# Linear attention and an MLP in one kernel: decay row through TensorE, matmuls of the identity in the opening, group 0 in smaller pieces, other load gates and order keys

## The chip, the cores and the metric

One core of a Trainium2 chip. The metric is the device time in microseconds (us) of one execution; the median of some runs stands for a kernel.

## What is computed

Inputs r, k, v of shape (4, 8, 768, 48), f32, and w, u of shape (8, 48). For each of 4 batches and 8 heads, over 768 steps:

```python
cur = outer(u * k_t, v_t)
y_t = r_t @ (state + cur)
state = w[:, None] * state + outer(k_t, v_t)
```

y, seen as 3072 tokens of 384 columns, goes through an MLP: h = x @ w_in (384 x 2048), a gate g (h where h >= 1, 0 where h <= -1, (h + 1)^2 / 4 between), and out = g @ w_out (2048 x 384), f32.

## The kernel before

Time is cut into 6 chunks of 128 steps. A group is one chunk of two batches, so there are 12 groups (g = 0 to 11) of two units each; a unit is 128 tokens. For a group, SP loads R, K and V (L268, L345). Four products follow (L273 to L313): Rs = R * Wup and Ks = K * Wdn, where Wup and Wdn are powers of w by the row's place in the chunk, KU = K * u, RKU = R * KU. `usum` adds RKU up by head (L318), and V2 (L320) is V times that sum. TensorE turns Rs and Ks (T, copied out as TT; from group 5 on by DMA transposes), multiplies them to A, which VectorE masks to AT (L385), and makes Y (from AT, V and the bf16 state) and Sp (the state's update). y = Y + V2 (L412) is turned to xT (TensorE for groups 0 to 2, a DMA transpose from group 3 on).

The MLP takes a group of 256 tokens in four quarters q: `mm1` is 12 matmuls into the PSUM tile hp (L487), ScalarE makes relu (L499) and square (L503), VectorE the gate (L507). Two hp tiles exist, so the third quarter waits for the first one's gate. `mm2` (L521) multiplies the gates by w_out into op, `o` copies op out, `out` stores it. TensorE's other results share four PSUM banks.

All operations are declared with `op` (L156): the engines that may run it with their assumed costs, a key, and what it needs, makes and uses. The loop from L564 on emits them one after the other: of the operations that could start within 0.25 us of the earliest, by assumed times, that with the lowest key on the same engine. Each engine runs its instructions in that emitted order and waits at each for what it really needs. Assumed times and `LOAD_AFTER` (L161) shape the order alone; real waits come from the tiles' buffers.

The opening: `w_row` and `u_row4` are set by memset and then partly loaded (L82 to L86); ScalarE takes the logarithm (L176), VectorE spreads it over the partitions (L179), ScalarE makes Wup and Wdn (L185, L188). w_col is loaded by columns (L92) and squared 7 times on VectorE (L192), for the state's decay wCm. Group 0's products go in halves of 384 columns, one per unit; its Rs and Ks are fixed to VectorE (L312), for groups 1 and 2 the planner chooses between GpSimd and VectorE, later groups use GpSimd.

The weights go in four pieces each through GpSimd's queue, cast to bf16 (L220, L226). `gate_on` (L216) is a 1x1 copy on GpSimd that reads a loaded tile and so holds back the pieces behind it: w_in 0 and 1 behind group 0's second R, w_in 2 and 3 behind group 1's K, w_out 0 and 1 behind group 2's R, w_out 2 and 3 behind group 2's K (L213, L214).

Of the kernel before, what the change touches and what calls it, by code (L numbers as in the profile page):

```python
# [22 lines left out]
def kernel(  # L23
# [53 lines left out]
    w_row = const.tile([P, DM], F32, name="w_row")  # L77
# [12 lines left out]
    for j in range(2):  # L90
        src = bass.AP(tensor=w.tensor, offset=w.offset + j * D, ap=[[1, D], [2 * D, NP]])
        nc.scalar.dma_start(out=w_col[j * HP : j * HP + D, :], in_=src)  # L92
# [28 lines left out]
    lw_row = const.tile([P, DM], F32, name="lw_row")  # L121
    lw = const.tile([P, DM], F32, name="lw")
# [23 lines left out]
    }  # L146
    FLEX, XDMA, TDMA, VCAST = 3, 3, 5, 12
# [30 lines left out]
    def lw_spread(e):  # L178
        nc.vector.stream_shuffle(lw, lw_row, [0] * QUAD)  # L179
# [4 lines left out]
    def wup(e):  # L184
        nc.scalar.activation(Wup.rearrange("p h d -> p (h d)"), lw, AF.Exp, scale=up_col, bias=0.0)  # L185

    def wdn(e):
        nc.scalar.activation(Wdn.rearrange("p h d -> p (h d)"), lw, AF.Exp, scale=dn_col, bias=0.0)  # L188
# [10 lines left out]
    op("w_row", (("NET", 0.0, 3.6),), -99, None)  # L199
    op("u_row4", (("NET", 0.0, 4.0),), -99, None)  # L200
    op("w_col", (("NET", 0.0, 5.0),), -99, None)
    op("lw_row", (("ACT", 0.55),), -98, lw_ln, ["w_row"])
    op("lw", (("DVE", 0.5, 0.08),), -98, lw_spread, ["lw_row"])
    op("u_bc", (("DVE", 0.5, 0.08),), -75, u_spread, ["u_row4"])
    op("exps", (("ACT", 1.28),), -98, lambda e: nc.scalar.preload_act_table_set("exp_and_others"), ["lw_row"])
    op("Wup", (("ACT", 0.53, 0.08),), -97, wup, ["lw", "exps"])
    op("Wdn", (("ACT", 0.53, 0.08),), -96, wdn, ["Wup"])
    op("w_power", (("DVE", 0.6),), -50, w_power, ["w_col"])
    op("wCm", (("ACT", 0.5),), -49, w_spread, ["w_power"])


    NW = 4
    GATE_IN = {0: ("R", 0, 1), 2: ("K", 1, 1)}  # L213
    GATE_OUT = {0: ("R", 2, 1), 2: ("K", 2, 1)}  # L214
    for i in range(NW):
# [10 lines left out]
        def w_out_go(e, i=i):  # L226
            n = slice(i * nF // NW, (i + 1) * nF // NW)
# [24 lines left out]
    for g in range(nG):  # L252
# [4 lines left out]
        for j0, j1 in parts:  # L257
# [5 lines left out]
            for i, (x, what) in enumerate(((r, "R"), (k, "K"))):  # L263

                def load(e, g=g, j0=j0, j1=j1, x=x, what=what):
                    if j0 == 0:
                        tiles[what, g] = loads.tile([P, UNITS * H, D], F32, name=what, tag=what)
                    nc.sync.dma_start(out=tiles[what, g][:, j0 * H : j1 * H, :], in_=source(x, g, j0, j1))  # L268

                op(f"load {what}{tag}", (("DMA", 0.9 * n, 1.35),), tl + i * 0.3, load, LOAD_AFTER.get((what, g), [f"load R{tag}"] if i else []),  # L270
                   [(what, (what, g))] if j0 == 0 else [], [(what, g)])
# [23 lines left out]
            pool_or_dve = (("POOL", 0.89 * n, 0.06, "PORT"), ("DVE", 0.03 + 0.49 * n, 0.05, "PORT")) if early_g else (("POOL", 0.89 * n, 0.06, "PORT"),)  # L295
            pool_only = (("POOL", 0.89 * n, 0.06, "PORT"),)
            first = j0 == 0
            for i, (what, needs) in enumerate(
# [11 lines left out]
                where = pool_or_dve if i < 2 or g in (0, 1, 2) else pool_only  # L310
                if g == 0 and i < 2:
                    where = (("DVE", 0.52, 0.05, "PORT"),)  # L312
# [25 lines left out]
        if g < VCAST:  # L338
# [8 lines left out]
            op(f"loadV{g}", (("DMA", 1.8, 1.35),), (-78 if g == 0 else t0 - 4 + 0.7 + shift("load", g)), load_v32, LOAD_AFTER.get(("V", g), [f"load K{g}.0"] if g else ["load K0.1"]), [("VF", ("VF", g))], [("VF", g)])  # L347
# [9 lines left out]
        for j in range(UNITS):  # L357
# [86 lines left out]
            if g < TDMA:  # L444
                op(f"T{n}", (("PE", 0.45, 0.17),), ka, t_in, [f"Rs{part}", f"Ks{part}"] + ([f"A{n - 1}"] if n > 3 else []), [("bank", ("T", n))], [("T", n), ("Rs", g), ("Ks", g)])
                op(f"TT{n}", (("ACT", 0.92, 0.1), ("DVE", 0.61, 0.08)) if n < 4 else (("DVE", 0.61, 0.08),), ka + 0.3, t_out, [f"T{n}"], [("TT", ("TT", n))], [("T", n), ("TT", n)])
            else:
                tt = f"KT{g}"
                if j == 0:
                    for i in range(2):  # L450
# [5 lines left out]
                        op(f"{'RK'[i]}T{g}", (("DMA", 1.4, 2.6),), ka - 2 + i, t_dma, [f"{w_}{part}"] + ([f"RT{g}"] if i else []),  # L456
# [21 lines left out]
            if g < XDMA:  # L478
                op(f"X{n}", (("PE", 0.17, 0.17),), ka + 3, x_mm, [f"y{n}"], [("bank", ("X", n))], [("X", n), ("y", n)])
                op(f"xT{n}", (("ACT", 0.38, 0.1),), ka + 3.1, x_out, [f"X{n}"], [] if j else [("xT", ("xT", g))], [("X", n), ("xT", g)])  # L480
            else:
                op(f"xT{n}", (("DMA", 0.5, 2.7),), ka + 3, x_dma, [f"y{n}"], [] if j else [("xT", ("xT", g))], [("y", n), ("xT", g)])

        for q in range(nQ):
            k1 = nQ * g + 3 + q + shift("mm1", g)

            def mm1(e, g=g, q=q):  # L487
                hp = tiles["hp", g, q] = psh.tile([P, FG, TOK], F32, name="hp", tag="h")
                for f in range(FG):
# [11 lines left out]
            def square(e, g=g, q=q):
                tiles["sq", g, q] = moe.tile([P, FG, TOK], F32, name="sq", tag="sq", bufs=2)
                nc.scalar.activation(tiles["sq", g, q], tiles.pop(("pt", g, q)), AF.Square, bias=0.0)  # L503

            def gate(e, g=g, q=q):
                gt = tiles["gt", g, q] = gpool.tile([P, FG, TOK], BF16, name="gt", tag="g")
                nc.vector.scalar_tensor_tensor(  # L507
                    out=gt, in0=tiles.pop(("sq", g, q)), scalar=1.0, in1=tiles.pop(("hp", g, q)), op0=ALU.min, op1=ALU.max
                )

            m = (g, q)
            op(f"mm1 {m}", (("PE", 1.31, 0.17),), k1, mm1, [f"xT{g * UNITS}", f"xT{g * UNITS + 1}", f"w_in{q * NW // nQ}"], [("h", ("hp", m))], [("hp", m), ("xT", g)])
            op(f"relu {m}", (("ACT", 0.93, 0.1),), k1 + 0.2, relu, [f"mm1 {m}"], [("pt", ("pt", m))], [("hp", m), ("pt", m)])
            op(f"square {m}", (("ACT", 0.965, 0.1),), k1 + 0.3, square, [f"relu {m}"], [("sq", ("sq", m))], [("pt", m), ("sq", m)])
            op(f"gate {m}", (("DVE", 1.135, 0.09),), k1 + 0.9 + shift("gate", g), gate, [f"square {m}"], [("g", ("gt", m))], [("hp", m), ("sq", m), ("gt", m)])

        for j in range(UNITS):
            for q in range(nQ):
# [13 lines left out]
                op(f"mm2 {o}{q}", (("PE", 0.65, 0.17),), k2, mm2, [f"gate {(g, q)}", f"w_out{q * NW // nQ}"] + ([f"mm2 {o}{q - 1}"] if q else []),  # L532
# [20 lines left out]
    free = {"POOL": 3.9, "DVE": 3.0, "DMA": 2.5}  # L553
# [10 lines left out]
    while waiting:  # L564
        found = []
        for name, (where, key, fn, needs, makes, uses) in waiting.items():
# [15 lines left out]
            for w in where:  # L582
                e = w[0]
                s = max([start, free.get(e, 0.0)] + [free.get(x, 0.0) for x in w[3:]] + [done[x][0] + HOP[e] if done[x][1] != e else done[x][2 if e == "DMA" else 0] for x in needs])
# [7 lines left out]
        cost = w[1] * (2 if e == "PE" and s < 17 else 1)  # L592
# [52 lines left out]
```

## Time and profile before

| | us |
|---|---|
| median of 3 runs | 198.72 |
| lowest, highest | 198.06, 200.79 |
| the profiled execution | 198.8 |
| its span in the trace | 197.0 |

PE is TensorE's matmuls, PEld its weight loads, DVE VectorE, ACT ScalarE, POOL GpSimd, SP the queue that issues loads and stores. The page cuts the span into 40 slices of 4.9 us; a digit is the busy share in tenths. A timeline row gives the start, the length, the engine, the line, the operation with out<-in, shapes, a count where equal ones are merged, and in brackets the idle time before it and what ended it. A row of windows gives the stretch and its length, the busy time of PE, PEld, DVE, ACT and POOL with the count of instructions, the granted clock of TensorE as a share of 2.4 GHz, the share of the DMA engines and GB/s.

### The profile page before, as it was taken

The numbers are of one execution on the slowest core, as the hardware profiler recorded it, in microseconds if no ns is written. First come the engines' busy times: TensorE is split into PE (matmuls) and PEld (weight loads), VectorE is DVE, ScalarE is ACT, GpSimd is POOL, SyncE is SP. The second block draws the span as 40 slices with busy tenths as digits, with TensorE's granted clock in tenths as the row PEclk, the third lists the DMA queues.
The fourth block names the chain that finished last, engine by engine and source line by source line (L and its number), as shares of the span: only waits on it lengthen the run. The fifth ranks groups of instructions, "written<-read, shape, count | busy, mean of one in ns | idle before, by whom it ended". The sixth has DMA issues, their size and how long they took to land.

```text
span 197.0 us, 4036 instructions
## 1 busy us (share of the span) xinstructions
PE 164.2 (83%) x1602; PEld 119.2 (61%) x1602; DVE 141.5 (72%) x205; ACT 134.6 (68%) x167; POOL 101.4 (51%) x82
## 2 busy tenths in 40 slices
PE   0064768299889989999694799999999999999992
PEld 0043656158667676767473477777777777777751
DVE  4699959966997979594780877797787867644540
ACT  2753398235978699775926698777976878878730
POOL 2303303084799888989974579999965000000000
PEclk9999999579999999999999799999999999999998
DMA  6999999999597999979989969744627311121112
GB/s 121 184 191 205 200 194 212 197 195 188 117 186 134 216 168 191 198 148 195 161 156 192 229 122 205 163 113 79 93 60 134 97 39 32 52 63 40 40 40 80
DMA packets 104226, 27.73 MB, mean 141 GB/s; under 512 B 97544, under 2 KB 104208, under 8 KB 104208
## 3 DMA queue, kind: packets, MB, share of 16 engines
q1 hardware_dynamic: 100064, 24.32, 68.8%
q0 software_dynamic: 3712, 3.15, 9.9%
q8 instruction: 12, 0.20, 0.4%
q10 hardware_dynamic: 432, 0.01, 0.2%
q14 instruction: 6, 0.05, 0.1%
HBM read 20.46 MB, written 4.72 MB: 128 GB/s over the span
## 4 chain that ended last, share of the span: by engine, by line
PE 48%; DMA 16%; DVE 13%; ACT 10%; POOL 5%; issue 4%; SPq 2%; POOLq 0%; DVEq 0%; ACTq 0%
PE op L526 21%; PE hp L492 21%; DMA VF<-in_v_dram 14%; ACT sq L503 4%; ACT pt L499 4%; DVE gt L507 3%; DVE AT L385 2%; PE A L380 2%; DMA R<-in_r_dram 2%; DVE Rs L287 1%; PE Y L407 1%; ACT state_bf L169 1%; ACT V L169 1%; POOL state L427 1%; DVE RKU L293 1%
## 5 line engine op out<-in xcount | busy, mean ns | idle before, releaser
L507 DVE SCALAR_TENSOR_TENSOR gt<-sq,hp 128x1024 bf16<-128x1024 f32 x48 | 58.4, 1216 | 33.0 <-ACT sq L503 32.9
L492 PE MATMUL hp<-xT,w_in_sb 128*128 128x256 bf16 x576 | 73.0, 278 | 9.4 <-DVE gt L507 8.7
L526 PE MATMUL op<-w_out_sb,gt 128*128 128x384 bf16 x384 | 75.6, 334 | 4.9 <-DVE TT L169 4.1
L492 PEld LDWEIGHTS <-w_in_sb 128*128 128x128 bf16 x576 | 57.1, 100 | 22.7 <-issue 11.1
L499 ACT ACTIVATE pt<-hp 128x1024 f32<-128x1024 f32 x48 | 48.9, 1018 | 14.8 <-PE hp L492 14.8
L503 ACT ACTIVATE sq<-pt 128x1024 f32<-128x1024 f32 x48 | 50.8, 1058 | 1.3
L526 PEld LDWEIGHTS <-gt 128*128 128x128 bf16 x384 | 35.1, 99 | 25.8 <-issue 6.9
L385 DVE TENSOR_TENSOR AT<-A,umask 128x512 bf16<-128x512 f32 x48 | 31.1, 683 | 8.7 <-PE A L380 8.5
L427 POOL TENSOR_TENSOR state<-Tm,wCm 128x384 f32<-128x384 f32 x16 | 16.0, 1001 | 13.7 <-DVE Tm L422 13.7
L287 POOL TENSOR_TENSOR Rs<-R,Wup 128x768 bf16<-128x768 f32 x9 | 16.4, 1821 | 7.9 <-DMA R<-in_r_dram 7.9
L169 ACT CAST state_bf<-state 128x384 bf16<-128x384 f32 x20 | 10.2, 508 | 15.0 <-DVE state L424 9.0
L169 ACT CAST V<-VF 128x768 bf16<-128x768 f32 x12 | 10.0, 833 | 14.2 <-DMA VF<-in_v_dram 14.2
L289 POOL TENSOR_TENSOR Ks<-K,Wdn 128x768 bf16<-128x768 f32 x9 | 16.4, 1819 | 0.5 <-PE Y L407 0.5
L293 POOL TENSOR_TENSOR RKU<-R,KU 128x768 f32<-128x768 f32 x9 | 16.3, 1816 | 0.4
L291 POOL TENSOR_TENSOR KU<-K,u_bc 128x768 f32<-128x768 f32 x9 | 16.4, 1823 | 0.0
L323 POOL TENSOR_TENSOR V<-V,diag 128x768 f32<-128x768 bf16 x9 | 13.3, 1477 | 4.7 <-DVE y L414 2.7
L414 DVE TENSOR_TENSOR y<-Y,V 128x384 bf16<-128x384 f32 x24 | 13.2, 551 | 0.3
L169 ACT COPY o_sb<-op 128x384 f32<-128x384 f32 x22 | 10.2, 464 | 4.5 <-PE op L526 4.5
L369 PE MATMUL T<-ident,Rs 128*128 128x128 bf16 x40 | 4.6, 246 | 10.3 <-DVE Rs L287 10.2
L318 DVE TENSOR_REDUCE diag<-RKU 128x16 f32<-128x768 f32 (+1 forms) x13 | 11.5, 886 | 1.4 <-POOL RKU L293 1.3
L407 PE MATMUL Y<-V,AT 128*128 128x48 bf16 x192 | 11.9, 188 | 0.2
L407 PEld LDWEIGHTS <-AT 128*128 128x128 bf16 x192 | 10.2, 99 | 1.3 <-issue 0.6
(59 smaller groups left out, 117.0 us busy)
## 6 DMA issues: line engine op xcount, KB each, us to landing
VF<-in_v_dram SPq DMA_DIRECT2D x12, 384.0 KB, 5.9
out_dram<-o_sb SPq DMA_DIRECT2D x24, 192.0 KB, 2.1
R<-in_r_dram SPq DMA_DIRECT2D x11, 384.0 KB, 5.7
K<-in_k_dram SPq DMA_DIRECT2D x11, 384.0 KB, 6.1
w_in_sb<-in_moe_w_in_dram POOLq DMA_DIRECT2D x4, 384.0 KB, 7.3
w_out_sb<-in_moe_w_out_dram POOLq DMA_DIRECT2D x4, 384.0 KB, 8.5
R<-in_r_dram SPq DMA_DIRECT2D x2, 192.0 KB, 3.6
K<-in_k_dram SPq DMA_DIRECT2D x2, 192.0 KB, 4.1
```

The lines of the kernel that those rows point to most:

```text
L169: nc.scalar.copy(out, in_) if e == "ACT" else engines[e].tensor_copy(out, in_)
L287: engines[e].tensor_mul(part(R_s)[:, :, :, :D], part(R), rep(Wup, j1 - j0))
L289: engines[e].tensor_mul(part(K_s)[:, :, :, :D], part(K), rep(Wdn, j1 - j0))
L293: engines[e].tensor_mul(part(tiles["RKU", g]), part(R), part(tiles["KU", g]))
L385: nc.vector.tensor_mul(tiles["AT", n][:, i], tiles["A", n][i], umask.unsqueeze(1).to_broadcast([P, NP, P]))
L407: nc.tensor.matmul(Y[:, 2 * p + i, :], AT[:, i, p, :], V[:, j * H + 2 * p + i, :], start=(c == 0), stop=True, skip_group_check=True,)
L427: nc.gpsimd.tensor_mul(states[b], tiles.pop(("Tm", n)), wCm)
L492: nc.tensor.matmul(hp[:, f, :], w_in_sb[:, i, n0 : n0 + P], tiles["xT", g][:, i, :], start=(i == 0), stop=(i == nK - 1), skip_group_check= ...
L499: nc.scalar.activation(tiles["pt", g, q], tiles["hp", g, q], AF.Relu, bias=0.5, scale=0.5)
L503: nc.scalar.activation(tiles["sq", g, q], tiles.pop(("pt", g, q)), AF.Square, bias=0.0)
L507: nc.vector.scalar_tensor_tensor(out=gt, in0=tiles.pop(("sq", g, q)), scalar=1.0, in1=tiles.pop(("hp", g, q)), op0=ALU.min, op1=ALU.max)
L526: nc.tensor.matmul(tiles["op", g, j], tiles["gt", g, q][:, f, j * P : (j + 1) * P], w_out_sb[:, n, :], start=(n == 0), stop=(n == nF - 1),)
```

## The change

In the opening w_row becomes one partition. TensorE spreads its logarithm with a matmul against a row of ones, and makes w_col with eight small matmuls; the two w_col loads go. `fill` emits 128x128 matmuls of the identity into a spare hp tile wherever the planner sees TensorE free for over 0.5 us before the first `mm1`. Group 0's `mm1` goes in four pieces (half of the rows of hp by unit), its relu, square and gate in two halves. Rs and Ks of group 0 may run on GpSimd too. The gates are fewer: all of w_in behind group 0's second R, all of w_out behind group 1's K. `TUNE` adds an offset to the key of every kind of operation by group (0 to 3, 10, 11, and m for 4 to 9), `ONLY` fixes the engine of some (index into the list of allowed ones). The assumed costs of loads, transposes and products change. TT, xT of groups 0 to 2 and o may run on either of ScalarE and VectorE.

```diff
-    w_row = const.tile([P, DM], F32, name="w_row")
+    w_row = const.tile([1, DM], F32, name="w_row")
-    nc.vector.memset(w_row, 1.0)
+    nc.scalar.dma_start(out=w_row, in_=bcast(w, 1))
+    nc.vector.memset(ones, 1.0)
-    nc.scalar.dma_start(out=w_row[0:P:QUAD, :], in_=bcast(w, P // QUAD))
...
-        nc.scalar.dma_start(out=w_col[j * HP : j * HP + D, :], in_=src)
...
+    TUNE = {
...
+        'KU': {0: 25.13, 1: 33.08, 2: -2.32, 3: 3.63, 11: 0.46, 'm': 13.06},
...
+        'V': {0: 3.19, 2: -4.04, 3: 0.92, 10: 2.53, 11: -0.93, 'm': 12.34},
...
+    ONLY = {
+        'KU': {1: 1, 2: 1},
+        'Ks': {0: 1, 1: 1, 2: 1},
+        'RKU': {0: 0, 2: 1},
+        'Rs': {0: 1},
+        'TT': {1: 0, 2: 0, 'm': 0},
+        'V2': {0: 0, 1: 0, 2: 1},
+        'o': {1: 0, 10: 1, 11: 0, 2: 0, 3: 0},
+        'w_power': {0: 1},
+        'xT': {0: 0, 1: 0, 2: 1},
+    }
...
-    LOAD_AFTER = {("R", 1): ["w_in1"], ("R", 2): ["w_in3"], ("R", 3): ["w_out3"]}
+    LOAD_AFTER = {("R", 1): ["w_in3"], ("R", 2): ["w_out3"]}
...
-        nc.vector.stream_shuffle(lw, lw_row, [0] * QUAD)
+        nc.tensor.matmul(tiles["lw"], ones, lw_row, start=True, stop=True)
...
+                nc.tensor.matmul(
+                    tiles["wc"][j * HP : j * HP + D, p : p + 1], w_row[:, h * D : (h + 1) * D], ones[:, :1],
...
-    GATE_IN = {0: ("R", 0, 1), 2: ("K", 1, 1)}
-    GATE_OUT = {0: ("R", 2, 1), 2: ("K", 2, 1)}
+    GATE_IN = {0: ("R", 0, 1)}
+    GATE_OUT = {0: ("K", 1, 1)}
...
-                if g == 0 and i < 2:
-                    where = (("DVE", 0.52, 0.05, "PORT"),)
+                where = pool_or_dve
...
-            op(f"loadV{g}", (("DMA", 1.8, 1.35),), (-78 if g == 0 else t0 - 4 + 0.7 + shift("load", g)), load_v32, LOAD_AFTER.get(("V", g), [f"load K{g}.0"] if g else ["load K0.1"]), [("VF", ("VF", g))], [("VF", g)])
+            op(f"loadV{g}", (("DMA", 2.1, 1.35),), (-78 if g == 0 else t0 - 4 + 0.7 + shift("load", g)), load_v32, LOAD_AFTER.get(("V", g), [f"load K{g}.0"] if g else ["load K0.1"]), [("VF", ("VF", g))], [("VF", g)])
...
+            pieces = [(f, j) for f in range(2) for j in range(UNITS)] if g == 0 else [(None, None)]
+            runs = [slice(0, 2), slice(2, FG)] if g < FINE else [slice(0, FG)]
...
+    WARM = (2.2, 22.0)
+    def fill(n):
+        if "warm" not in tiles:
+            tiles["warm"] = psh.tile([P, FG, TOK], F32, name="warm", tag="h")
+        for _ in range(n):
+            nc.tensor.matmul(tiles["warm"][:, 0, :P], ident, ident, start=True, stop=True, skip_group_check=True)
...
-        cost = w[1] * (2 if e == "PE" and s < 17 else 1)
+        cost = w[1]
+        if e == "PE":
+            spare = s - free.get(e, WARM[0])
+            if s < WARM[1] and spare > 0.5 and ("hp", 0, 0) not in tiles:
+                fill(int((spare - 0.2) / 0.11))
```

## Rows read from the trace of the kernel before

**Rows 1.** The page's 40 slices: TensorE's busy tenths, the DMA share

```profile
PE   0064768299889989999694799999999999999992
...
DMA  6999999999597999979989969744627311121112
```

**Rows 2.** Busy time in windows, by stage, and one of the opening

```profile
21.27:45.27 24.00, 17.91 (x159) 12.64 (x159) 18.86 (x24) 13.67 (x17) 9.00 (x9) 0.86 1.25 200
45.27:117.43 72.16, 64.42 (x678) 47.45 (x676) 53.73 (x74) 53.75 (x68) 57.75 (x38) 0.98 0.98 173
...
8.84:20.15 11.31, 5.74 (x59) 3.82 (x59) 11.14 (x23) 4.96 (x8) 1.72 (x3) 1.00 1.32 196
```

**Rows 3.** Timeline around group 5's w_in matmuls; first ones of groups 6, 11

```profile
99.39 1.48 PE L492 MATMUL hp<-xT,w_in_sb 128*128 128x256 bf16 x12
...
105.10 0.83 ACT L169 CAST V<-VF 128x768 bf16<-128x768 f32 x1 [5.53 <-DMA VF<-in_v_dram]
...
109.66 1.98 PE L492 MATMUL hp<-xT,w_in_sb 128*128 128x256 bf16 x12 [3.90 <-DVE gt L507]
...
117.43 0.82 PE L492 MATMUL hp<-xT,w_in_sb 128*128 128x256 bf16 x6
...
177.75 1.47 PE L492 MATMUL hp<-xT,w_in_sb 128*128 128x256 bf16 x12
```

**Rows 4.** Timeline of TensorE: first w_in matmuls, first w_out ones, group 1's first

```profile
21.27 2.72 PE L492 MATMUL hp<-xT,w_in_sb 128*128 128x256 bf16 x12 [0.57 <-ACT xT L169]
24.63 1.73 PE L492 MATMUL hp<-xT,w_in_sb 128*128 128x256 bf16 x12
38.20 2.72 PE L526 MATMUL op<-w_out_sb,gt 128*128 128x384 bf16 x8 [4.11 <-DVE TT L169]
45.27 1.47 PE L492 MATMUL hp<-xT,w_in_sb 128*128 128x256 bf16 x12
```

**Rows 5.** Timeline of the opening, ScalarE and VectorE

```profile
5.07 0.52 ACT L176 ACTIVATE lw_row<-w_row 128x384 f32<-128x384 f32 x1 [0.80 <-DMA w_row<-in_w_dram]
6.91 0.61 ACT L185 ACTIVATE Wup<-lw,up_col 128x384 f32<-128x384 f32 x1
7.57 1.34 DVE L192 TENSOR_TENSOR w_col<-w_col 128x4 f32<-128x4 f32 x7 [0.88 <-DMA w_col<-in_w_dram]
8.84 0.55 DVE L291 TENSOR_TENSOR KU<-K,u_bc 128x384 f32<-128x384 f32 x1
18.73 0.94 DVE L287 TENSOR_TENSOR Rs<-R,Wup 128x768 bf16<-128x768 f32 x1
```

**Rows 6.** Timeline of VectorE behind group 2's products

```profile
36.59 0.96 DVE L323 TENSOR_TENSOR V<-V,diag 128x768 f32<-128x768 bf16 x1
39.19 0.68 DVE L385 TENSOR_TENSOR AT<-A,umask 128x512 bf16<-128x512 f32 x1
```

**Rows 7.** Windows after TensorE's two long holes

```profile
38.20:42.00 3.80, 3.80 (x20) 1.95 (x20) 3.80 (x6) 0.49 (x1) 2.40 (x2) 0.50 1.05 199
110.00:113.60 3.60, 3.60 (x25) 2.03 (x23) 3.05 (x6) 1.79 (x4) 2.92 (x3) 0.56 1.29 221
```

**Rows 8.** Waits, whole span: total, times, longest

```profile
ACT V L169 <- DMA VF<-in_v_dram: 14.2, 7, 5.5
```

**Rows 9.** GpSimd's gate and group 3; w_out and group 3's R to landing

```profile
29.24 0.17 POOL L218 COPY gone<-K 1x1 f32<-1x1 f32 x1 [5.81 <-DMA K<-in_k_dram]
...
w_out_sb<-in_moe_w_out_dram POOLq DMA_DIRECT2D x4, 384.0 KB, 8.5
...
L268 SPq DMA_DIRECT2D R<-in_r_dram x1: 6135/6135/6135, 23.4 to 23.4; - x1
...
DMA to landing us min/median/max: 15.5/15.5/15.5
...
39.07 1.81 POOL L287 TENSOR_TENSOR Rs<-R,Wup 128x768 bf16<-128x768 f32 x1 [7.90 <-DMA R<-in_r_dram]
...
53.62 1.48 POOL L323 TENSOR_TENSOR V<-V,diag 128x768 f32<-128x768 bf16 x1 [1.41 <-DVE diag L318]
```

More of the change, by code (lines that the diff above doesn't have):

```diff
@@ L1 @@
+import re
 from contextlib import ExitStack
@@ new lines, with stage @@
+    ONLY = {
[8 more added lines that the diff above has]
+        'xT': {0: 0, 1: 0, 2: 1},
+    }
+    PER_UNIT = ("T", "TT", "A", "AT", "Sp", "Tm", "decay", "sbf", "Y", "y", "X", "xT")
+    def stage(name):
+        kind = re.match(r"([A-Za-z_ ]+)", name).group(1).strip() + ("!" if name.endswith("!") else "")
+        if re.match(r"V2\d+\.", name):
+            return "V2", int(name[2:].split(".")[0])
+        if kind.startswith("load"):
+            kind = "load"
+        if kind in ("RT", "KT"):
+            kind = "RKT"
+        n = re.search(r"\((\d+), ", name) or re.search(r"(\d+)", name)
+        n = int(n.group(1)) if n else 0
+        return kind, n // UNITS if kind in PER_UNIT else n
@@ L153, with tuned @@
+    def tuned(name, where, key):
+        kind, g = stage(name)
+        g = "m" if 4 <= g < nG - 2 else g
+        pick = ONLY.get(kind, {}).get(g)
+        if pick is not None and len(where) > 1:
+            where = (where[pick],)
+        return where, key + TUNE.get(kind, {}).get(g, 0.0)
     ops = {}
@@ L184, in wup, with w_take @@
     def wup(e):
-        nc.scalar.activation(Wup.rearrange("p h d -> p (h d)"), lw, AF.Exp, scale=up_col, bias=0.0)
+        nc.scalar.activation(Wup.rearrange("p h d -> p (h d)"), tiles["lw"], AF.Exp, scale=up_col, bias=0.0)
     def wdn(e):
-        nc.scalar.activation(Wdn.rearrange("p h d -> p (h d)"), lw, AF.Exp, scale=dn_col, bias=0.0)
+        nc.scalar.activation(Wdn.rearrange("p h d -> p (h d)"), tiles["lw"], AF.Exp, scale=dn_col, bias=0.0)
+    def w_take(e):
+        for j in range(2):
+            rows = slice(j * HP, j * HP + D)
+            nc.vector.tensor_copy(w_col[rows, :], tiles["wc"][rows, :])
     def w_power(e):
@@ L268, in load @@
                     nc.sync.dma_start(out=tiles[what, g][:, j0 * H : j1 * H, :], in_=source(x, g, j0, j1))
[L270 removed]
+                op(f"load {what}{tag}", (("DMA", (0.95 if g == 0 else 1.05) * n, 1.35),), tl + i * 0.3, load, LOAD_AFTER.get((what, g), [f"load R{tag}"] if i else []),
                    [(what, (what, g))] if j0 == 0 else [], [(what, g)])
@@ L501, in square, with relu @@
[L501 to L506, printed above, removed]
+            def relu(e, g=g, q=q, x=0, fs=None):
+                if x == 0:
+                    tiles["pt", g, q] = moe.tile([P, FG, TOK], F32, name="pt", tag="pt", bufs=2)
+                nc.scalar.activation(tiles["pt", g, q][:, fs], tiles["hp", g, q][:, fs], AF.Relu, bias=0.5, scale=0.5)
@@ L511 @@
[L511 to L515, printed above, removed]
+                    out=tiles["gt", g, q][:, fs], in0=tiles["sq", g, q][:, fs], scalar=1.0, in1=tiles["hp", g, q][:, fs],
@@ new lines, in gate @@
+                    op0=ALU.min, op1=ALU.max,
+                )
+            for z, (f, j) in enumerate(pieces):
+                xs = [f"xT{g * UNITS + x}" for x in (range(UNITS) if j is None else [j])]
+                op(f"mm1 {m}{z}", (("PE", 1.31 / len(pieces), 0.17),), k1 + 0.05 * z, lambda *x, fn=mm1, f=f, j=j, z=z: fn(*x, f=f, j=j, first=not z),
+                   xs + [f"w_in{q * NW // nQ}"] + ([f"mm1 {m}{0}"] if z else []), [] if z else [("h", ("hp", m))], [("hp", m), ("xT", g)])
+            nr = len(runs)
@@ new lines @@
+            for x, fs in enumerate(runs):
+                part = dict(x=x, fs=fs)
+                have = [f"mm1 {m}{z}" for z, (f, j) in enumerate(pieces) if nr == 1 or f is None or f == x]
+                one = [] if x else [("pt", ("pt", m))], [] if x else [("sq", ("sq", m))], [] if x else [("g", ("gt", m))]
+                op(f"relu {m}{x}", (("ACT", 0.08 + 0.85 / nr, 0.1),), k1 + 0.2 + 0.05 * x, lambda e, fn=relu, p=part: fn(e, **p),
+                   have + ([f"relu {m}0"] if x else []), one[0], [("hp", m), ("pt", m)])
+                op(f"square {m}{x}", (("ACT", 0.11 + 0.855 / nr, 0.1),), k1 + 0.3 + 0.05 * x, lambda e, fn=square, p=part: fn(e, **p),
+                   [f"relu {m}{x}"] + ([f"square {m}0"] if x else []), one[1], [("pt", m), ("sq", m)])
+                op(f"gate {m}{x}", (("DVE", 0.07 + 1.065 / nr, 0.09),), k1 + 0.9 + 0.05 * x + shift("gate", g), lambda e, fn=gate, p=part: fn(e, **p),
+                   [f"square {m}{x}"] + ([f"gate {m}0"] if x else []), one[2], [("hp", m), ("sq", m), ("gt", m)])
@@ L552 @@
     left = dict(users)
-    free = {"POOL": 3.9, "DVE": 3.0, "DMA": 2.5}
+    free = {"POOL": 3.9, "DVE": 3.0, "DMA": 2.0}
     done = {}
@@ L583 @@
                 e = w[0]
-                s = max([start, free.get(e, 0.0)] + [free.get(x, 0.0) for x in w[3:]] + [done[x][0] + HOP[e] if done[x][1] != e else done[x][2 if e == "DMA" else 0] for x in needs])
+                s = max([start, free.get(e, 0.0)] + [free.get(x, 0.0) for x in w[3:]] + [done[x][0] + HOP[e] if done[x][1] != e else done[x][2 if e in ("DMA", "POOL") else 0] for x in needs])
                 if best is None or s + w[1] < best[0] + best[4][1]:
```

121 lines of the change are left out of this document (79 added, 42 removed), and 17 rows, old and new, of the table TUNE.

## Prediction

> **What bounds the kernel now.** I read the page's slices first [rows 1]: TensorE has next to nothing to do in the first tenth of the span, is full from about slice 23 on, and between the two it has holes, while the DMA row stands at 9 for nearly all of slices 2 to 23. The windows by stage [rows 2] turn this into a sum. From 117.43 to the start of the last group at 177.75 [rows 3] TensorE runs five groups without a hole: 60.32 / 5 = 12.06 us per group. That stretch can't be helped by an order. What lies before it can: 21.27 us until the first w_in matmul [rows 4]; 24.00 us until group 1's first one at 45.27, in which TensorE does one group; four groups in 54.12 us up to 99.39 (13.53 each); one group in 18.04 us up to 117.43. Against 12.06 each, that is some 12 us lost in the second stretch, 5.9 in the third and 6.0 in the fourth, and nearly all of the first.
>
> What holds TensorE differs by stage, which the timeline and the waits show. In the opening it is VectorE: from 8.84 to 20.15 it is busy 11.14 of 11.31 us [rows 2]. Before 8.84 it computes w_col to the 128th power for 1.34 us, after a wait for a transfer [rows 5]. In the second stretch TensorE waits 4.11 us at 38.20 for VectorE's copy of TT [rows 4]. VectorE had just run group 2's chain of products, whose last starts at 36.59, and so AT of group 1's second unit, without which group 1 has no xT, comes only at 39.19 [rows 6]. After that idle time the granted clock is 0.50 (1.2 GHz) from 38.20 to 42.00 [rows 7]. In the fourth stretch ScalarE stands 5.53 us in front of a V cast whose load has not landed; the relus behind it come late and TensorE waits 3.90 us for the gate at 109.66 [rows 3], and 110.00 to 113.60 again runs at about half clock (0.56) [rows 7]. Such waits for V add up to 14.2 us in 7 places [rows 8].
>
> The profiled execution is 198.8 us, 1.8 us more than its span of 197.0; it is 0.1 us above the median of the three times shown, so I subtract from 198.8.
>
> **The change part by part.**
>
> *(a) Opening, until the first w_in matmul: -4.6 us.* The w_row transfer no longer waits for a memset, and the powers of w no longer wait for the w_col transfers: TensorE makes that column from w_row, so the 1.34 us of powers move into time in which VectorE waits for Ln and Wup anyway. Today the first product starts at 8.84, though Wup runs from 6.91 to 7.52 [rows 5]. KU needs no Wup and Rs can follow it, so I let the products begin at about 6.9: -1.9 us. Spreading the logarithm through TensorE costs between one matmul of 384 columns in bf16 (2.72 us for eight, 0.34 us [rows 4]) and eight times that for f32 at a low clock, 2.7 us (an estimate: no f32 matmul is in the trace). ScalarE's second table load lies between Ln (5.07 to 5.59) and Wup (6.91) in the meantime, so that the near end is free and the far end puts Wup some 1.4 us later. I take nothing, as those 1.3 us of cover are about the middle of the two. Next, RKU and V2 of group 0 go to GpSimd: four halves of about 0.55 us (KU's half at 8.84 is of that kind) [rows 5], 2.2 us off VectorE; and group 1's Rs, 0.94 us at 18.73 [rows 5], now stands ahead of group 0's last y only if its load is in, which the four w_in pieces make later. That is 3.1 us, but GpSimd issues four w_in transfers first and takes about 0.74 us for half of the 1.48 us V2 [rows 9], so the first y may come to wait for it: I count -2.5. With the clock up, X and what is around it gain 0.2. Bounds: -1 (GpSimd late, f32 matmul dear) to -7 (VectorE's chain also loses KU and the AT gaps).
>
> *(b) Group 0's own MLP: -1.1 us.* The identity matmuls fill TensorE's gaps until the first w_in matmul. Twelve of those take 2.72 us at 21.27, 1.73 at 24.63 and 1.47 at 45.27 [rows 4]: with the higher clock from the first, 1.25 + 0.26 us. The half-quarters let the first relu start after half of the matmuls, some 0.7 us earlier. They double the fixed part of each relu, square and gate: 2 x 0.55 - 0.96 = 0.14 us for a product of 384 against 768 columns [rows 5, 6], eight times on ScalarE, 1.1 us. Net -1.1, bounds -2.2 and +1.5 (the upper: a fill still running when the data is there, and the clock not up).
>
> *(c) From group 0 to group 1: -5.0 us.* The stall of 4.11 us, and 1.9 us for 3.80 us at half clock [rows 4, 7], are together 6.0. They go if AT of group 1 no longer stands behind group 2's products. The diff gives the products of groups 0 to 2 new keys, puts some on GpSimd, which idles until group 3's R is in [rows 9], and has V2 of group 1 there. It does not say in which place each lands, so the bounds are 0 and -6, and I take -5 because GpSimd alone can relieve VectorE by one to three operations of 0.96 us. For w_out: today its third and fourth piece stand behind a gate that opens at 29.24, and land some 8.5 us after their issue, at about 38 and 39 [rows 9], which would be the next bound. All four now follow group 1's K, so I take this cover for given. Group 1 then starts at 45.27 - 4.6 - 1.1 - 5.0 = 34.6.
>
> *(d) The stall at 109.66: -3.0 us.* 18.04 - 12.06 = 6.0 us hang on one V cast placed too early. The keys of V in the middle groups grow by 12.34, and the planner's prices of loads and transposes are raised, so that it expects V later. Whether this cast is the one that moves can't be seen: half.
>
> *(e) Groups 1 to 4, the tail, and what is queued: 0.* The V waits speak for a gain, at most the 5.9 us that this stretch loses; that TensorE will want its data 11 us earlier from a DMA that is no faster speaks for a loss, which I bound by the same figure. The end after 177.75 keeps its 19.25 us, give or take 1. The TT, xT and o copies that change engines I leave at nothing.
>
> Sum: 198.8 - 4.6 - 1.1 - 5.0 - 3.0 = 185.1.
>
> **The rivals.**
>
> *1. The front's gain is given back to the DMA: 194.8.* The DMA share is 1.25 and the rate 200 GB/s from 21.27 to 45.27 [rows 2]; group 3's R, issued at 23.4, needs 15.5 us to land [rows 9], and GpSimd starts group 3 on it at 39, ending with V2 at 53.62 + 1.48 [rows 9]. V2 is followed by y, xT and then group 3's w_in matmuls, which I put some 5 us later, at about 60; today they start near 45.27 + 2 x 13.53 = 72. So group 3 can be at most 12 us earlier. If four w_out pieces go ahead of R (4 x 384 KB at 200 GB/s are 7.9 us), 4 us are left: 198.8 - 4 = 194.8. For it: the DMA row [rows 1]. Against it: the same bytes are ahead of R today. The Trainium skill has a rule here ("DMA: Bandwidth & Descriptors", section "Issuing engines are not separate DMA queues"): transfers from all issuing engines run on the same 16 DMA engines and interleave, so pulling weights forward on GpSimd's queue is paid by SP's loads. The rate, 200 GB/s with both queues in use against 173 with SP's alone later, agrees so far; by the rule alone the sum would be this rival's.
>
> *2. The middle gets better too: 177.* All of (c) and (d) at their far ends and 4 us in (e): 198.8 - 4.6 - 1.1 - 6.0 - 6.0 - 4.0 = 177.1. For it: the V waits [rows 8] are waits of an order, since V's data is wanted only groups later. Against it: an order that fits the chip at every place.
>
> *3. Slower, ScalarE stands in front of V more often: 204.* Each V cast that still stands ahead of a relu finds its load no earlier than now (the DMA is full up to slice 23) while ScalarE is there up to 13 us sooner; the wait then eats the front's gain whole. Each such stall lets the clock fall as after 109.66, for 3.60 us at 0.56, 1.6 us lost [rows 7]. Three in place of one, with the split costs of (b): 198.8 + 2 x 1.6 + 1.5 = 203.5, say 204. It decides from three V casts on that are placed before the relu of a group three earlier. The raised load prices speak against it.
>
> *4. The change doesn't do what it says:* the fills leave the clock low, and VectorE's queue in group 1 stays as it is: (a) at -1, (c) at 0, (d) at -3: 195; it shares its time with rival 1.
>
> **How the numbers follow.** Forecast 0.50 (own range 180 to 190); rivals 1 and 4 together 0.26; rival 2 0.16; rival 3 0.08. From 177 to 197 leaves out half of rival 2, rival 3 and a little of 1: 2 in 10. Two per cent, about what a measurement of this kernel tells from no change, is 4.0 us, so faster means under 194.7: all of the forecast and of rival 2, and a little over half of rivals 1 and 4: 0.80. Slower than 202.7 is most of rival 3: 0.06. The rest, 0.14, is no change.
>
> **What would show it.** Right: first w_in matmuls near 17 us with twelve of them near 1.5 us; group 1's first near 35; no idle time of 4 us before the first w_out matmul and no stretch at 0.50 after it; V waits on ScalarE well below 14.2 us. (a) is wrong if VectorE's first product still begins after 8 us, or TensorE waits for GpSimd's V2. (c) is wrong if group 1's AT still runs near 39. The prediction as a whole is wrong if group 1 starts near 35 and yet the span moves by less than 5 us (rival 1), or ScalarE's waits for V grow (rival 3).

## The result and the profile after

After: 189.06 us, the median of four executions (188.73 to 191.38), before beside it 198.53; the ratio is 0.953, interval 0.942 to 0.963. The forecast was 185.1 with 177 to 197. The profiled execution took 189.0 us, its span 187.2. Medians here and below are of all executions, while ratios and intervals compare only those in the faster of two states into which executions of one kernel fall.

The slices of the page after (TensorE, its granted clock, the DMA share) answer to [rows 1]:

```profile
PE   5967847999998999999999999999998989999992
PEclk9995665589999999999999999999999999999999
DMA  6999999931989989899989879798698941210032
```

Counted from 0, TensorE shows no digit under 8 from slice 7 to 38, where before had 6, 4 and 7 in slices 19, 21 and 22. The clock row shows 5 and 6 in slices 3 to 7. The windows by stage, answering to [rows 2]:

```profile
15.03:38.42 23.39, 17.98 (x167) 14.87 (x166) 14.80 (x23) 14.85 (x26) 4.62 (x6) 0.57 1.24 194
38.42:59.62 21.20, 20.11 (x199) 14.12 (x198) 15.33 (x21) 14.74 (x19) 10.93 (x8) 0.99 0.66 129
59.62:96.00 36.38, 36.19 (x402) 27.38 (x401) 31.45 (x43) 33.39 (x41) 34.82 (x23) 1.00 1.04 170
96.00:168.00 72.00, 70.66 (x718) 52.38 (x716) 59.68 (x79) 58.05 (x65) 47.53 (x32) 1.00 0.71 148
```

From 59.62 to 168 TensorE is busy 106.85 of 108.38 us. Ahead of that little is better: group 0's stretch lasts 23.39 us where it lasted 24.00, at a mean clock of 0.57 in place of 0.86. Group 1's stretch, busy by the digits, has 199 matmuls in 21.20 us where the stretch behind it has 402 in 36.38.

Where the time went is read best from the first relu of each group (ScalarE's timeline):

| us | g0 | g1 | g2 | g3 | g4 | g5 | g6 | g8 | g11 | end |
|---|---|---|---|---|---|---|---|---|---|---|
| before | 24.0 | 46.8 | 61.9 | 73.7 | 87.2 | 106.2 | 119.5 | 144.5 | 179.3 | 198.8 |
| after | 17.1 | 40.1 | 61.1 | 72.9 | 86.0 | 97.1 | 108.1 | 132.9 | 168.3 | 189.0 |
| lead | 6.9 | 6.7 | 0.8 | 0.8 | 1.2 | 9.1 | 11.4 | 11.6 | 11.0 | 9.8 |

The opening wins 6.9 us, group 1 loses 5.9 of it, and the two groups 4 and 5 win 10.2. The gain of the whole is, in this pair, that of the middle.

The opening, from the timeline:

```profile
3.23 0.52 ACT L254 ACTIVATE lw_row<-w_row 1x384 f32<-1x384 f32 x1
3.80 1.64 PE L258 MATMUL lw<-lw_row,ones 1*128 1x384 f32 x2 [0.39 <-ACT lw_row L254]
5.48 0.58 ACT L274 ACTIVATE Wup<-lw,up_col 128x384 f32<-128x384 f32 x1 [0.43 <-PE lw L258]
6.09 1.02 DVE L382 TENSOR_TENSOR Rs<-R,Wup 128x384 bf16<-128x384 f32 x2 [0.43 <-ACT Wup L274]
...
15.03 2.08 PE L591 MATMUL hp<-xT,w_in_sb 128*128 128x128 bf16 x18
...
38.42 2.77 PE L591 MATMUL hp<-xT,w_in_sb 128*128 128x256 bf16 x22
```

The spread through TensorE is a matmul in f32 (two instructions in the trace) of 1.64 us. It lies beside ScalarE's table load, outlasts it, and Wup waits 0.43 us for it. The first product starts at 6.09, not 8.84. The chain of the opening then runs through GpSimd:

```profile
6.16 3.19 POOL w_in_sb L319 x4
9.36 0.02 issue
9.38 1.01 POOL RKU L388
10.39 0.95 POOL KU L386
11.34 0.04 issue
...
11.42 1.00 POOL RKU L388
```

Four w_in issues, then the products of group 0, then V2 and y: GpSimd is the bound here now. And the 18 matmuls of 128 columns at 15.03 take 2.08 us; where the clock is full they take 1.44 (below). In this execution the identity matmuls did not keep it up.

Behind group 1 the trace shows this, on VectorE, SP and GpSimd:

```profile
42.28 1.22 DVE L609 SCALAR_TENSOR_TENSOR gt<-sq,hp 128x1024 bf16<-128x1024 f32 x1 [4.57 <-ACT sq L604]
43.42 0.95 DVE L382 TENSOR_TENSOR Rs<-R,Wup 128x768 bf16<-128x768 f32 x1
...
49.14 0.95 DVE L415 TENSOR_TENSOR V<-V,diag 128x768 f32<-128x768 bf16 x1
```

```profile
27.49 8.08 SPq L363 DMA_DIRECT2D R<-in_r_dram  x1
44.65 0.36 SPq L654 DMA_DIRECT2D out_dram<-o_sb  x1
45.10 1.42 SPq L363 DMA_DIRECT2D K<-in_k_dram  x1
...
50.34 1.82 POOL L384 TENSOR_TENSOR Ks<-K,Wdn 128x768 bf16<-128x768 f32 x1 [8.55 <-DMA K<-in_k_dram]
```

Group 2's products stand behind group 1's first gate and VectorE idles 4.57 us ahead of it; group 3's K stands behind group 0's first store on SP, so that GpSimd waits 8.55 us. The DMA row has its hole there (slices 8 and 9). That is where the lead of 6.7 us ends. The chain that ended last runs from that gate through VectorE's products of group 2 (43.42 to 50.09), and not through GpSimd's wait for K; that these places cost the lead is read from the trace and was not tried by moving them.

### The profile page after: what moved, and what is told of

Its sections match the earlier page's. It is cut to its first block, busy times and chain, and to the rows that moved or that the text cites. A ratio compares the mean times of both kernels' runs of the same rounds, so it can differ in the third digit from the quotient of the medians.

```text
span 187.2 us, 4259 instructions
## 1 busy us (share of the span) xinstructions
PE 171.4 (92%) x1713; PEld 127.3 (68%) x1713; DVE 140.1 (75%) x209; ACT 136.5 (73%) x169; POOL 107.0 (57%) x86
## 4 chain that ended last, share of the span: by engine, by line
PE 64%; DVE 11%; ACT 8%; POOL 7%; issue 6%; DMA 2%; SPq 1%; POOLq 0%; DVEq 0%; ACTq 0%
PE hp L591 29%; PE op L639 26%; DVE gt L609 5%; PE A L472 3%; ACT pt L599 3%; DMA K<-in_k_dram 2%; POOL RKU L388 2%; ACT sq L604 2%; DVE AT L477 2%; PE Y L499 2%; POOL w_in_sb L319 2%; ACT TT L247 2%; POOL KU L386 1%; PE Sp L484 1%; PE T L461 1%
## 5 line engine op out<-in xcount | busy, mean ns | idle before, releaser
L591 PE MATMUL hp<-xT,w_in_sb 128*128 128x256 bf16 (+1 forms) x624 | 74.7, 276 | 5.5 <-DVE gt L609 4.0
L609 DVE SCALAR_TENSOR_TENSOR gt<-sq,hp 128x1024 bf16<-128x1024 f32 (+1 forms) x52 | 58.8, 1133 | 24.4 <-ACT sq L604 18.0
L591 PEld LDWEIGHTS <-w_in_sb 128*128 128x128 bf16 x624 | 60.6, 104 | 17.4 <-issue 7.2
L599 ACT ACTIVATE pt<-hp 128x1024 f32<-128x1024 f32 (+1 forms) x52 | 49.6, 954 | 16.8 <-PE hp L591 16.7
L604 ACT ACTIVATE sq<-pt 128x1024 f32<-128x1024 f32 (+1 forms) x52 | 51.6, 992 | 1.6
L415 POOL TENSOR_TENSOR V<-V,diag 128x768 f32<-128x768 bf16 (+1 forms) x12 | 16.3, 1365 | 8.2 <-ACT V L247 6.6
L388 POOL TENSOR_TENSOR RKU<-R,KU 128x768 f32<-128x768 f32 (+1 forms) x11 | 18.4, 1670 | 0.7
L386 POOL TENSOR_TENSOR KU<-K,u_bc 128x768 f32<-128x768 f32 (+1 forms) x10 | 17.4, 1741 | 0.0
L247 ACT COPY o_sb<-op 128x384 f32<-128x384 f32 x14 | 6.5, 470 | 8.3 <-PE op L639 7.6
L247 ACT COPY TT<-T 128x1024 bf16<-128x1024 bf16 x8 | 8.1, 1010 | 2.8 <-PE T L461 2.8
```

Source lines behind the costliest of these rows:

```text
L247: nc.scalar.copy(out, in_) if e == "ACT" else engines[e].tensor_copy(out, in_)
L386: engines[e].tensor_mul(part(tiles["KU", g]), part(K), rep(u_row, j1 - j0))
L388: engines[e].tensor_mul(part(tiles["RKU", g]), part(R), part(tiles["KU", g]))
L591: nc.tensor.matmul(hp[:, f, cols], w_in_sb[:, i, n0 : n0 + P], tiles["xT", g][:, i, cols], start=(i == 0), stop=(i == nK - 1), skip_group_ ...
L599: nc.scalar.activation(tiles["pt", g, q][:, fs], tiles["hp", g, q][:, fs], AF.Relu, bias=0.5, scale=0.5)
L604: nc.scalar.activation(tiles["sq", g, q][:, fs], tiles["pt", g, q][:, fs], AF.Square, bias=0.0)
```

## The experiments

Twelve runs, each beside the kernel before on the same chip.

**1. The clock: no_fill, fills_on, fills_more.** No identity matmuls; then such matmuls in every gap that the planner sees up to 40 us; then 1.6 times as many.

```diff
-            if s < WARM[1] and spare > 0.5 and ("hp", 0, 0) not in tiles:
...
+            elif 7.0 <= s < 40.0 and spare > 0.12:
+                many = int(1.0 * (spare - 0.06) / 0.058)
...
```

> The changed kernel without the identity matmuls; the order is the same. In the changed kernel the granted clock is about half from 15 to 38 us although the fills ran before. Theory (the fills raise the clock only up to group 0's first w_in matmul): the first w_in matmul comes 0.5 to 1.5 us later than 15.03, the matmuls after it take as long as now, and the time is 189 to 190.5. Rival (the fills are worth what the prediction's step b gave them and more): 191 to 193.

> The changed kernel with identity matmuls in every gap that the planner sees on TensorE from 7 to 40 us, also after group 0's first w_in matmul; the order is the same. Theory (the low clock from 15 to 38 lies on the chain and costs the front most of what it had gained): the clock stays near full, group 1's first w_in matmul moves from 38.4 to 33 to 35, the time falls to 185 to 187. Rival (the front waits for data, not for TensorE): group 1 stays within 1 us of 38.4 and the time within 1 us of 189.

> As the run before, with 1.6 times as many identity matmuls in each gap. Theory (low clock): if the plain filling leaves holes in which the clock falls, this one closes them: group 1 at 33 to 35 and 185 to 187 even where the first does not reach it. Rival: TensorE gets later at each step by what is filled too much, 189 to 192.

Measured: 189.42 us (ratio 0.948, 0.930 to 0.966) without any; 189.16 (185.04 to 189.32; no interval) with all; 192.38 (0.970, 0.962 to 0.978) with more. Without fills the first relus of groups 0 and 2 come at 17.9 and 61.7 us: the fills are worth nothing that shows. With fills throughout, the window and the first w_in matmuls of groups 0 and 1 are

```profile
15.00:37.00 22.00, 19.78 (x312) 17.27 (x311) 16.72 (x27) 15.79 (x27) 5.45 (x7) 1.00 1.23 191
```

```profile
17.31 0.50 PE L591 MATMUL hp<-xT,w_in_sb 128*128 128x128 bf16 x6
...
35.62 2.56 PE L591 MATMUL hp<-xT,w_in_sb 128*128 128x256 bf16 x22
```

The clock is full, group 1 starts 2.8 us earlier, though group 0 starts 2.3 later, and group 2's first relu comes at 60.2 in place of 61.1, with the same end. So group 0's stretch takes 18.31 us at full clock and 23.39 in the profiled execution of after: the low clock costs some 5 us there (the two orders differ by the fills alone), and in these two executions they are given back by the end. That a full clock wins nothing at all is not shown: one of the four executions of *fills_on* took 185.04 us, 3.7 less than the fastest of after, and no trace of it was kept. More fills only stand in the way (group 1's first relu at 43.0).

**2. The V casts: before_v_late.** The kernel before, with the casts of V of groups 6 to 10 held until after the last relu of the group four earlier; no other instruction moves.

```diff
+    HOLD = {f"V{g}": f"relu {(g - 4, 3)}" for g in range(6, 11)}
...
+        if name in HOLD:
+            kept[HOLD[name]] = (fn, e)
...
```

> The kernel before; only the V casts of groups 6 to 10 come later on ScalarE, each behind the last relu of the group four earlier. Theory (the gain of the change in the middle is ScalarE no longer standing in front of V): the holes of 1.8 and 3.9 us on TensorE before 96 and 109.7 go, and with them the half clock after 110; group 6 starts 5 to 7 us earlier and the time is 191.5 to 193.5. Rival (V is only where the delay shows; the loads, products or the front set it): 197.5 to 199.

Measured: 198.94 us, ratio 0.999 (0.992 to 1.006). The waits from 59 to 125 us show why, first one of before, then two of before_v_late:

```profile
ACT V L169 <- DMA VF<-in_v_dram: 13.1, 6, 5.5
...
PE hp L492 <- DMA xT<-y: 5.0, 3, 2.9
...
ACT V L169 <- DMA VF<-in_v_dram: 0.3, 1, 0.3
```

ScalarE's waits for V went from 13.1 us (6 times) to 0.3 in this stretch, and the hole only moved: TensorE now waits for xT, a transpose that SP issues.

```profile
111.39 0.56 DVE L414 TENSOR_TENSOR y<-Y,V 128x384 bf16<-128x384 f32 x1
113.11 1.20 SPq L476 DMA_TRANSPOSE xT<-y  x1
```

SP issues the transposes of xT at 105.32, 113.11 and 119.72 us, where before it issued them at 104.62, 111.99 and 119.62: its queue kept its times to within 1.2 us, whatever ScalarE did. The wait that ended last was not the one that bound.

**3. The searched order: before_m, no_m, no_tune.** The offsets of the middle alone put into before; taken out of after; all offsets and fixed engines taken out of after.

```diff
-    TUNE = {
...
+    TUNE = {}
+    ONLY = {}
```

> The kernel before with one part of the change alone: the offsets of the searched order for the middle groups (4 to 9, the entries 'm'); opening, gates, group 0 and the offsets of groups 0 to 3, 10 and 11 stay as before. Theory 'the middle of the order makes the gain': the hole of groups 4 and 5 goes, the first relu of group 6 comes some 8 us earlier than the 119.5 of before, the time is 189 to 193 us. Rival 'the hole goes because the groups ahead of it come in another rhythm, the front and groups 1 to 3': the hole stays, 197 to 201 us.

> The kernel after with the offsets of the middle groups (4 to 9) set to nothing, all else as changed. Theory 'the middle of the order makes the gain': the first relus of groups 0 and 1 stay at 17 and 40 us and that of group 5 falls back from 97 to 102 to 106, the time to 195 to 199 us, as before. Rival 'the front makes it': 188 to 192 us.

> The kernel after with all offsets and all fixed engines of the searched order taken out: what is left are the decay row by TensorE, the identity matmuls, group 0 in half-quarters, the gates and the new costs of the planner. Theory 'the searched order makes the gain': 196 to 201 us. Rival 'the edits of the opening and of group 0 make it': 188 to 193 us.

Measured: 200.9 us beside 200.05 of before; 193.3 (0.968, 0.961 to 0.976); 190.28 (0.954, 0.947 to 0.961). So 178 offsets and 23 fixed engines are worth about 1 us over none, inside the intervals, and the middle's offsets alone do nothing that shows in before (no interval could be given for it). With those of the middle taken out the time is longer than with none, so these go with the others; *front_tune* below, which keeps only those of groups 0 to 2, is as fast as none. Without any, the first relus of groups 2 and 3 are no earlier than before (61.9 and 73.7 there):

```profile
61.92 1.02 ACT L546 ACTIVATE pt<-hp 128x1024 f32<-128x1024 f32 x1 [0.94 <-PE hp L538]
...
74.10 1.02 ACT L546 ACTIVATE pt<-hp 128x1024 f32<-128x1024 f32 x1
```

And yet the end is some 8 us earlier in these two traces: from group 2 on a group takes an even 11.2 to 12.4 us. What made the middle even was thus neither a lead of the front nor the search.

**4. What the opening is worth: late_opening.**

```diff
+        for _ in range(6):
+            nc.scalar.activation(junk, junk_in, AF.Ln, bias=0.0)
         nc.scalar.activation(lw_row, w_row, AF.Ln, bias=0.0)
```

> The kernel after with six 128x1024 logarithms ahead of the decay row's on ScalarE, some 6 us of added work at its start (its result is not used), order else the same. Theory 'what the opening gains is given back by group 2': the first relu of group 0 comes some 4 us later (21), that of group 2 within 1 us of 61, the time 189 to 191 us. Rival 'a us won in the opening is a us of the time': 192.5 to 195 us.

Measured: 192.94 us (0.968, 0.959 to 0.977), 3.9 above after. First w_in matmuls of groups 0 and 1:

```profile
21.90 1.44 PE L596 MATMUL hp<-xT,w_in_sb 128*128 128x128 bf16 x18
...
41.35 3.64 PE L596 MATMUL hp<-xT,w_in_sb 128*128 128x256 bf16 x24
```

6.9 us later at the start, 2.9 at group 1, 3.3 at group 2 (64.4), 3.9 at the end. That 6.9 became 2.9 is the clock: group 0's stretch ran at a mean of 0.87 here, 0.57 after. Beside *no_m*, which differs in the middle's offsets and whose front ran at 0.87 too (19.45 us in both), this run is 6.9 us late at the start, 6.9 at group 1 and 5.9 at group 2. "Given back by group 2" falls in this direction: what is late there stays late. Whether being earlier wins nothing is less sure. In *fills_on* an earlier group 1 was lost again by group 2, but *no_m* and *front_tune* reach group 2 at 58.5 and 58.1, ahead of after's 61.1, and lose the lead behind it with other orders of the middle; no bound at group 2 is shown.

**5. The planner's costs of transfers: before_dma, no_tune_olddma.** Four corrected costs alone, in before; and the old ones put back into no_tune.

```diff
-(("DMA", 0.9 * n, 1.35),)
+(("DMA", (0.95 if g == 0 else 1.05) * n, 1.35),)
-(("DMA", 1.8, 1.35),)
+(("DMA", 2.1, 1.35),)
-(("DMA", 1.4, 2.6),)
+(("DMA", 1.4, 3.0),)
-(("DMA", 0.5, 2.7),)
+(("DMA", 1.2, 2.0),)
```

Of each line only the cost is printed: those of a load of R or K, of V, of the transposes RT and KT, and of xT's.

> The kernel before with one part of the change alone: the four corrected costs of transfers by which the planner orders SP's queue (a load of R or K 1.05 us and 0.95 in group 0 for 0.9, of V 2.1 for 1.8, R's and K's transpose 3.0 us to land for 2.6, xT's transpose 1.2 and 2.0 us for 0.5 and 2.7); nothing else of the change. Theory 'these costs make the middle's gain, since loads no longer run a group ahead of the transposes on SP': no stretch between the first relus of groups 4 and 6 over 13.5 us (before 19.0 and 13.3), the time 190 to 194 us. Rival 'they only go with the new front, or the middle's gain has another cause': the hole stays or moves, 197 to 201 us.

> The kernel after without the searched order (as no_tune, 190.28 us), and with the costs of transfers of before put back. Theory 'the costs make the middle's gain': holes of over 14 us for one group come back behind group 3, the time 196 to 201 us, about that of before. Rival: the middle stays even (12.2 to 12.4 us a group) and the time is 189 to 193 us.

Measured: 192.25 us (0.970, 0.942 to 0.997) and 199.4 (1.001, 0.994 to 1.009). By the ratio an edit that changes no instruction, only their order, makes some 6 us in before, where the whole change made 9.4. Its interval is wide (0.6 to 11.6 us), so that its size stays uncertain, and the stretch of 13.5 us a group that was expected at most between the first relus of groups 4 and 6 was just missed (14.0 and 13.7). The other direction is clear: all else of the change without it, and without the search, makes none, 199.4 us where *no_tune* had 190.28, and the two intervals (0.994 to 1.009, 0.947 to 0.961) stand well apart. Windows 59 to 96 and 96 to 125 of before, before_dma and no_tune_olddma, in this order:

```profile
59.00:96.00 37.00, 34.48 (x358) 25.34 (x353) 28.30 (x38) 29.58 (x38) 33.75 (x23) 1.00 1.01 179
96.00:125.00 29.00, 25.10 (x242) 17.91 (x240) 19.60 (x27) 19.45 (x24) 20.93 (x15) 0.94 1.01 180
```

```profile
59.00:96.00 37.00, 36.57 (x403) 27.76 (x401) 31.39 (x43) 30.36 (x40) 36.68 (x26) 1.00 0.97 175
96.00:125.00 29.00, 26.85 (x278) 19.44 (x276) 20.67 (x27) 22.85 (x29) 22.69 (x15) 1.00 0.90 169
```

```profile
59.00:96.00 37.00, 34.81 (x372) 25.80 (x370) 29.19 (x39) 27.26 (x34) 36.23 (x24) 1.00 1.09 187
96.00:125.00 29.00, 26.75 (x261) 19.47 (x261) 24.71 (x34) 22.85 (x26) 22.49 (x16) 0.94 1.07 189
```

The old costs give a DMA share over 1.0 and fewer matmuls (600 and 633 in the two stretches), the new ones a lower share and 681. SP's timeline shows what a transfer does to its neighbours. Before, a y on VectorE and SP's issues behind it:

```profile
90.44 0.55 DVE L414 TENSOR_TENSOR y<-Y,V 128x384 bf16<-128x384 f32 x1
90.74 0.53 SPq L268 DMA_DIRECT2D R<-in_r_dram  x1
91.32 1.37 SPq L268 DMA_DIRECT2D K<-in_k_dram  x1
...
92.83 4.02 SPq L453 DMA_TRANSPOSE RT<-Rs  x1
...
96.96 1.20 SPq L476 DMA_TRANSPOSE xT<-y  x1
```

y is done at 90.99, and its transpose is issued at 96.96: 5.97 us in SP's queue behind two loads and a transpose whose issue alone takes 4.02. In before_dma:

```profile
98.15 0.55 DVE L414 TENSOR_TENSOR y<-Y,V 128x384 bf16<-128x384 f32 x1
98.72 1.19 SPq L476 DMA_TRANSPOSE xT<-y  x1
...
103.96 0.55 DVE L414 TENSOR_TENSOR y<-Y,V 128x384 bf16<-128x384 f32 x1
104.54 1.21 SPq L476 DMA_TRANSPOSE xT<-y  x1
```

0.02 and 0.03 us. Added up over the rows from 59 to 96 us, SP spends 35.1 of 37 us issuing before, 32.9 in no_tune_olddma, 31.3 in before_dma, 28.3 after and 25.7 in no_tune. From 96 to 125 us the share no longer parts the kernels: 25.4 of 29 us before and 18.5 in before_dma, but 24.3 in no_tune_olddma and 24.2 in no_tune. The Trainium skill names this bound in "Perfetto Trace Analysis", section "What "DMA-bound" means": a kernel can be bound by the issuing engine's sequencer, whose track is then solid with DMA slices. The trace of before agrees, with 35.1 of 37 us from 59 to 96; the page looks for the remedy in larger descriptors, and here the order alone was one.

The old plan took xT's transpose for 0.5 us of the queue; its issue takes 1.2. It put loads where it saw room, up to two groups further ahead: the last load of V is issued at 120.9 us before, at 122.0 in no_tune_olddma, at 142.4 in before_dma, 138.7 in no_tune and 144.8 after. The two early ones are the two slow kernels and the three late ones the three fast; among the three the time does not follow this number. Nor does the gain hang on one lucky order: the four kernels planned with the old costs (before, *before_m*, *before_rk2* below, *no_tune_olddma*) took 198.5 to 200.9 us, the five planned with the new ones (after, *no_m*, *no_tune*, *front_tune*, *before_dma*) 189.1 to 193.3.

**6. Loads alone: before_rk2.** Is it that the loads run too far ahead?

```diff
-    space = {"bank": 4, "h": 2, "R": 3, "K": 3, "V": 5, "VF": 2, ...
+    space = {"bank": 4, "h": 2, "R": 2, "K": 2, "V": 5, "VF": 2, ...
```

> The kernel before with all its costs, and the planner alone told that R and K have two buffers each (the kernel keeps three), so that a load of R or K is put on SP's queue later, and the costs of the transposes stay as they were. Theory 'what costs the middle of before is that loads run too far ahead on SP and fill the DMA engines': the last loads are issued later than the 116 to 121 us of before, the hole of groups 4 to 6 (87.2 to 119.5 us) shrinks by 3 us or more, the time is 192 to 196 us. Rival 'the corrected cost of the transposes made the gain of before_dma': 197 to 201 us.

Measured: 200.07 us, ratio 1.007 (1.002 to 1.012): a miss. The last load of V moved to 133.3 us and xT's delay behind y to at most 2.8 us, yet the first relus of groups 4 and 6 come at 92.5 and 119.3. The waits from 59 to 125 us:

```profile
ACT V L169 <- DMA VF<-in_v_dram: 9.6, 4, 4.5
```

With V's casts in their old places V now comes late for them. Holding loads of R and K back by itself is not the gain. Nor was a shorter issuing time on SP enough here: it is 30.2 of 37 us from 59 to 96, less than in *before_dma*. Which of the four costs is needed, and whether the transposes' prices or the even pace do it, stays open.

**7. A version of both: front_tune.** The offsets for groups 0 to 2 alone, the planner's own keys behind.

```diff
...
-        'KU': {0: 25.13, 1: 33.08, 2: -2.32, 3: 3.63, 11: 0.46, 'm': 13.06},
+        'KU': {0: 25.13, 1: 33.08, 2: -2.32},
...
```

> The kernel after with the offsets of the searched order kept for groups 0 to 2 alone; the rest runs by the planner's own keys, as in no_tune, where a group took an even 12.2 to 12.4 us. If what the opening wins is kept once the middle is even: first relus of groups 0 to 3 near 17, 37, 58 and 69 us as in no_m, groups of 12.3 us behind, and 184 to 187 us, faster than both kernels. If group 2's late loads or the middle give it back: 188 to 191 us.

Measured: 189.99 us (0.958, 0.939 to 0.977), no better than after. Its profiled execution, with a higher clock in group 0's stretch, is 4 us ahead at groups 1 and 3 (36.0 and 68.7); group 3 then takes 14.4 us, at group 5 2.0 us are left, and at group 8 none.

## Why the prediction was right, and where not

The sign, the interval and almost the size held; the terms did not, and that the sum is near is in good part luck. In this pair it came to -6.2, -0.6 and -2.95 where -4.6, -6.1 and -3.0 had been written.

*(a) -4.6:* the first w_in matmul came 6.2 us earlier, inside the bounds. The powers moved into the wait ahead of Wup (1.34 us at 3.82), as argued, and the products start at 6.09 (6.9 was forecast). The f32 matmul lay, as assumed, beside the table load; the factor of eight in its upper price came from no row, and it took 1.64 us, between the two ends of 0.34 and 2.7. The loss feared on GpSimd is there (w_in issues for 3.19 us), only smaller than allowed.

*(b) and (c) together -6.1:* 23.39 - 24.00 = -0.6 us. The step that failed in (b) is "with the higher clock from the first": in the profiled execution the clock fell as group 0's own matmuls began (0.98 from 13 to 15.03 us, 0.50 from 15.03 to 20) and stayed near 0.5 but for 20 to 25 us (0.82), and the 1.5 us of gain became a loss of some 5, by *fills_on*. In (c) the stall of 4.11 us did go, but the half clock that I took to end with it spread over the stretch. Where the clock stood, (b) and (c) came near their forecast: 18.31 - 24.00 = -5.7 us in *fills_on*, with group 1 at 35.6 where 34.6 was written. That gain was not kept: the end of that execution is that of after. The text named a front won without the span as the mark of rival 1, and the place is as it said: group 3's R took 8.08 us to issue, its K came 8.55 us late for GpSimd. That this is what ended the lead is not shown, since the chain goes by VectorE there. The Trainium skill's rule named there ("DMA: Bandwidth & Descriptors", section "Issuing engines are not separate DMA queues") fits that place, with the DMA share at 1.24; its sum, 194.8, fails, since the middle has a gain of its own.

*(d) -3.0 by the V cast, (e) 0:* the two together came to (189.0 - 38.42) - (198.8 - 45.27) = -2.95, by accident: group 1 to 2 lost 5.9, groups 4 and 5 won 10.2, the tail lost 1.2. The cause given in (d) is wrong: the cast's wait of 5.53 us was what the trace named, and removing all such waits moved nothing (*before_v_late*). The edit that acts was named in (d) in half a sentence ("the planner's prices of loads and transposes are raised") and priced by what it does to V. It should have been weighed by SP's queue, whose rows were not read: an xT that stands six microseconds behind its y, and a transpose planned at 0.5 us whose issue takes 1.2. That the four prices make the gain is shown by the runs; by which of them, and through what in the queue, stays open.

Rival 2 had the middle right in kind (a better order, no faster part) and its size of 10 us for (d) and (e); it did not have the loss at group 1. Rival 3 was wrong: ScalarE's waits for V fell from 14.2 to 4.9 us. Of rival 4's conditions one was met in the profiled execution (the fills leave the clock low), without its time.

## What to carry to other kernels

Where a planner orders the work, check each of its assumed costs against the trace, queues for transfers first: here, in the changed kernel without its search, four numbers decided between 199.4 and 190.3 us. Read the issuing queue's own timeline, from the end of the producer to the issue of its transfer, before blaming the engine whose wait ended last; a wait on an in-order engine may only be the place where lateness shows. And try a gain at the front in both directions: here a front that came later was paid for to the end, while fronts that came earlier won no median below that of after.

## What was not expected of the hardware

The clock of the front is a matter of the execution. In *no_m* and *front_tune*, with the same identity matmuls in the opening (23 from 7 to 15 us in *no_m* as in after), the 18 first matmuls ran at full clock:

```profile
14.99 1.44 PE L590 MATMUL hp<-xT,w_in_sb 128*128 128x128 bf16 x18
```

That is *no_m*, beside 2.08 us after and 2.17 in *no_fill*. What decides it was not found. Over the four executions of after the mean clock went from 0.944 to 0.991, and the time did not follow it (191.38 us at 0.944, 189.0 at 0.945, 188.73 at 0.991). A load of 384 KB whose issue on SP took 0.39 to 0.59 us in more than half of the cases after took 8.08 at 27.49, in the stretch whose DMA share is 1.24.
